# One PSUM bank for both query parts' sums, one for two second-layer products, two early score chunks in the ring banks, and new instruction orders

## The chip, the cores and the metric

The kernel runs on one core of a Trainium2 chip. The metric is device microseconds from start to end of one launch. Before the change the median of three runs is 324.44 us (324.27 to 324.97).

## What is computed

Attention for 8 batches, 8 heads, 576 queries of 64 elements, over 16 beacon keys and 576 causal keys; then a two-layer network on the 4,608 tokens, whose activation is h times the logistic function of 1.702 h.

```python
def _attn_ref(q, k, v, beacon_k, beacon_v):            # q, k, v: (8, 8, 576, 64)
    k_all = np.concatenate([beacon_k, k], axis=2)      # 16 beacon rows first
    v_all = np.concatenate([beacon_v, v], axis=2)
    scores = scale * np.matmul(q, k_all.transpose(0, 1, 3, 2))
    ...
    scores = np.where(causal, -1000000000.0, scores)
    a = np.exp(scores - scores.max(-1, keepdims=True))
    a /= a.sum(-1, keepdims=True) + 1e-09
    return np.matmul(a, v_all)
...
h = x @ w_in                                           # (4608, 512) @ (512, 2048)
g = h * (1.0 / (1.0 + np.exp(-1.702 * h)))
return g @ w_out                                       # (4608, 2048) @ (2048, 512)
```

## The kernel before

**Sets and chunks.** A set is four heads of one batch; there are 16. The scores of a set are kept transposed (keys on the partitions), only the blocks that the mask leaves, 1,664 columns for each head. They are made in 55 chunks (`CHUNKS`), of up to 512 columns for each of the four heads. For one chunk, PE runs 32-row matmuls (`e_qk`, L484) into four score banks of PSUM (tile s), and ScalarE takes the exponential of all four heads (`e_exp`, L495). The next chunk waits for that exponential, since there is one set of score banks (`chunk`, L933). Diagonal blocks are masked by GpSimd, those of the first halves of sets 0 and 1 by VectorE (`e_mask`, L509 and L516).

**Early and late sets.** Sets 0 to 3 are early: each half of the 288 queries has its own first chunk. Sets 4 to 15 are late and are worked off whole, in query parts of 224 and 352. For the softmax's denominators PE multiplies the exponentials by ones (`e_av` with x = 2, L571), for a late set after VectorE has added up the key blocks (`e_zadd`, L534). A late set's sums go to two ring banks, one for each query part. VectorE transposes each (`e_z1`, L583), takes reciprocals (L590) and transposes them back (`e_z2`, L594). The value products (`e_av` with x = 0 and 1, 32-column matmuls, L571) are multiplied by them into xT (`e_norm`, L606).

**The ring.** Four banks of PSUM, u0 to u3, are the ring: sums, value products, blocks of both layers all pass through them. An operation opens a bank, and its last reader closes it. After the last chunk the four score banks join the ring (`MORE`).

**The two layers.** Tokens go in groups of 256 (0 and 1) and 512 (2 to 9). The first layer runs in `e_m1` (L630), for groups 7 to 9 with seven products instead of eight (`e_part`, L831). The second layer is plain for groups 0 and 1 (`e_m2`, L675) and has seven products instead of eight for groups 2 to 9: `e_prod` (L744, 32 matmuls of 256 columns a product, in four operations), `e_half` (ScalarE, L755) and seven joins on VectorE (`e_join`, L760). Product 5 is joined twice, into u4 and into c22; c12 is u4 plus product 3. VectorE makes the products' left sides (`e_s`, L695).

**What sets the order.** `ORDER` lists for each engine the operations by number, the number being the place of the call of `op(...)` in the planning code. `Plan.run` follows the lists, gives every operation its ring bank, and the instructions are emitted engine by engine in that order. Each engine works off its own list in order. I call a PE operation score (mode r), value (c) or full (m); names are those of the planning code: qk7 is chunk 7, av1.2.0 the sums of set 1's first half (av1.0.0 and av1.1.0 its value products), m1.0.2 a block of group 0's first layer, m2.9.7.6 the last quarter of product 7 of group 9. On PE, the list of before begins:

qk0 qk1 av0.2.0 av0.0.0 av0.1.0 qk2 av1.2.0 av1.0.0 av1.1.0 qk3 m1.0.2 qk4 m1.0.0 qk5 m1.0.6 m1.0.4 av0.2.1 qk6 m1.0.8 m1.0.10 qk7 av0.1.1 m1.0.12 m1.0.14 m2.0.0.0 av1.2.1 av0.0.1 av1.0.1 av1.1.1 m2.0.0.1 m2.0.1.0 m1.1.0

On ScalarE: the exponentials of chunks 0 to 4 (chunks 0 and 1 in two instructions each), tanh twice, chunk 5, tanh twice, chunk 6. On VectorE: beacon cast, key transpose (the beacon's first), query transpose of set 0; the same of set 1; masks and normalisation of the first halves.

Of the kernel before, what the change touches and what calls it, by code (L numbers as in the profile page):

```python
# [7 lines left out]
F16 = mybir.dt.float16  # L8
# [9 lines left out]
        76, 100, 115, 118, 120, 106, 138, 141, 143, 108, 155, 111, 152, 129, 161, 158, 122, 131, 164, 167, 134, 127,  # L18
        170, 173, 176, 145, 125, 148, 150, 177, 182, 188, 191, 227, 194, 197, 232, 183, 203, 234, 200, 178, 237, 179,
        206, 258, 241, 209, 184, 263, 185, 212, 265, 213, 248, 246, 268, 214, 215, 401, 251, 253, 272, 218, 404, 275,  # L20
        244, 279, 219, 220, 407, 282, 284, 277, 221, 414, 320, 296, 304, 290, 302, 292, 300, 298, 312, 308, 294, 318,
        314, 310, 306, 316, 426, 435, 423, 343, 338, 339, 340, 433, 431, 438, 344, 345, 359, 349, 341, 464, 346, 350,
        351, 352, 354, 574, 355, 429, 360, 361, 577, 356, 362, 357, 372, 365, 583, 474, 477, 373, 366, 374, 367, 605,
        480, 484, 375, 482, 607, 368, 506, 502, 488, 492, 610, 490, 486, 498, 504, 500, 508, 514, 510, 516, 494, 496,
        512, 534, 593, 596, 535, 536, 539, 540, 550, 541, 542, 537, 742, 545, 546, 547, 548, 603, 745, 551, 552, 553,
        599, 601, 619, 622, 748, 555, 556, 557, 558, 561, 755, 625, 627, 629, 562, 563, 776, 568, 564, 569, 570, 571,
        779, 764, 767, 659, 637, 641, 657, 649, 651, 647, 661, 635, 631, 653, 805, 772, 770, 774, 643, 655, 633, 639,
        645, 679, 680, 815, 818, 700, 681, 682, 684, 701, 915, 690, 685, 686, 691, 692, 702, 918, 687, 693, 695, 703,
        696, 924, 821, 823, 697, 698, 706, 946, 825, 707, 713, 708, 709, 948, 934, 937, 714, 715, 716, 827, 951, 944,
        940, 942, 853, 831, 833, 855, 857, 851, 843, 835, 837, 847, 839, 845, 829, 849, 841, 1083, 960, 963, 875,  # L30
        876, 880, 877, 878, 881, 882, 1086, 968, 966, 970, 883, 1089, 902, 909, 903, 886, 891, 1096, 887, 888, 889,
        892, 893, 1117, 904, 894, 905, 896, 897, 1120, 898, 899, 910, 911, 1105, 1108, 1146, 912, 976, 994, 996, 972,
        978, 1000, 1002, 992, 984, 990, 986, 988, 974, 980, 982, 998, 1168, 1111, 1115, 1159, 1113, 1156, 1025, 1026,
        1020, 1027, 1171, 1021, 1022, 1028, 1023, 1031, 1177, 1032, 1033, 1164, 1166, 1162, 1199, 1034, 1036, 1047,
        1048, 1037, 1201, 1041, 1042, 1038, 1039, 1233, 1049, 1204, 1043, 1044, 1050, 1235, 1237, 1054, 1055, 1056,
        1057, 1239, 1249, 1190, 1241, 1265, 1251, 1242, 1253, 1255, 1187, 1245, 1267, 1258, 1281, 1257, 1269, 1216,
        1195, 1197, 1193, 1213, 1261, 1271, 1285, 1287, 1283, 1273, 1289, 1274, 1219, 1221, 1223, 1334, 1290, 1293,
        1277, 1357, 1335, 1313, 1318, 1314, 1336, 1315, 1319, 1316, 1320, 1321, 1373, 1324, 1325, 1337, 1326, 1329,
        1327, 1361, 1377, 1375, 1330, 1359, 1340, 1331, 1341, 1332, 1363, 1342, 1366, 1365, 1379, 1381, 1347, 1382,
        1348, 1369, 1389, 1385, 1349, 1343, 1395, 1393, 1391, 1405, 1350, 1397, 1398, 1409, 1437, 1407, 1411, 1413,  # L40
        1401, 1414, 1481, 1438, 1417, 1497, 1442, 1443, 1444, 1483, 1439, 1440, 1499, 1487, 1501, 1485, 1458, 1445,
        1459, 1460, 1489, 1513, 1490, 1448, 1453, 1449, 1450, 1451, 1454, 1503, 1455, 1493, 1505, 1461, 1456, 1464,
        1465, 1517, 1515, 1506, 1529, 1519, 1509, 1466, 1471, 1522, 1472, 1473, 1521, 1533, 1467, 1474, 1582, 1525,
        1535, 1537, 1531, 1538, 1561, 1566, 1562, 1541, 1588, 1567, 1589, 1563, 1564, 1568, 1569, 1572, 1590, 1573,
        1574, 1575, 1591, 1577, 1578, 1595, 1579, 1580, 1583, 1584, 1585, 1596, 1597, 1598,
    ],
    "ACT": [
        1, 3, 77, 79, 103, 101, 107, 109, 112, 153, 156, 130, 159, 162, 132, 165, 168, 135, 171, 174, 189, 192, 228,
        195, 198, 233, 235, 201, 204, 238, 180, 207, 259, 210, 264, 186, 266, 269, 216, 402, 405, 408, 222, 417, 415,
        297, 291, 303, 305, 301, 299, 293, 309, 321, 295, 319, 313, 315, 311, 307, 317, 436, 439, 342, 465, 468, 575,  # L50
        578, 584, 587, 606, 608, 503, 507, 489, 491, 493, 487, 499, 505, 509, 515, 517, 495, 501, 511, 497, 513, 611,
        538, 743, 746, 749, 756, 758, 777, 780, 660, 642, 638, 652, 658, 648, 650, 636, 632, 662, 654, 806, 644, 634,
        656, 640, 646, 809, 916, 683, 919, 928, 925, 947, 949, 952, 828, 832, 854, 856, 852, 858, 834, 838, 844, 840,
# [1304 lines left out]
```

## Time and profile before

| | |
|---|---|
| Median of three runs | 324.44 us |
| The profiled execution, and its span | 324.84 us, 323.1 us |
| Matmuls on PE | 4,508 |
| VectorE, ScalarE, GpSimd busy | 81%, 68%, 35% of the span |
| PE idle before its first matmul | 1.86 us |
| First score chunk, first first-layer matmul | 8.27 us, 17.21 us |
| Last matmul ends, last join ends | 319.06 us, 319.82 us |
| Loads of the first layer's weights land | 15.6 to 26.48 us |

The page gives each engine's busy time and its share of the span, and the span cut into 40 slices of some 8 us, with the busy share of each in tenths; the row PEclk is the clock that PE was granted. The chain of waits is the work that ended last, followed back from the end: start, length, engine, tile and line, and the number of matmuls merged into a piece. A row of the groups has line, engine, operation, what is written and read, the count, then busy time, the mean of one in ns, and the idle time ahead of them with what ended it. Timeline rows have start and length in us. Rows by window have busy times with instruction counts for PE, its weight loads, VectorE, ScalarE and GpSimd, then granted clock, DMA share and GB/s. PE's rows overlap, since matmuls are pipelined; the starts of single matmuls in the trace tell its pace.

### The profile page before, as it was taken

Reading aid. Unit: us, or ns where it says so; the run is one execution under the profiler, and the core shown is the slowest. Engines: PE = TensorE matmul, PEld = TensorE weight load, DVE = VectorE, ACT = ScalarE, POOL = GpSimd, SP = SyncE. Lnnn points to the kernel's source line nnn. Section 1 sums busy time; section 2 is a strip of 40 time slices with the busy share of each in tenths; the row PEclk is TensorE's granted clock in tenths of the full one; section 3 lists DMA queues with packets and bytes.
Section 4 is the critical chain, followed back from the end, with each engine's and each line's share of the span. In section 5 each row is a group of like instructions: output and inputs, shape, how many; then the busy total and the mean of one; then the engine's idle time right before and its main releaser. Section 6 shows DMA issues by size and latency. Waiting matters only on the chain. (4 is left out here: it accounts for less than half of the span.)

```text
span 323.1 us, 10371 instructions
## 1 busy us (share of the span) xinstructions
PE 312.2 (97%) x4508; PEld 230.0 (71%) x4508; DVE 261.7 (81%) x524; ACT 219.5 (68%) x272; POOL 113.4 (35%) x178
## 2 busy tenths in 40 slices
PE   7689999999999999999999999999999999999994
PEld 7467665644776467745878877646888888888884
DVE  4837798777987989976998889986999895585784
ACT  1676597677767686689767696768778735974830
POOL 8775478190328403871058208600221000000000
PEclk9899999999999999999999999999999999999998
DMA  7999999294423941396019908900111001101112
GB/s 124 163 200 208 206 185 184 54 97 85 123 70 66 185 73 34 53 183 89 2 36 134 189 3 80 176 28 2 37 34 65 4 32 34 67 2 36 65 67 97
DMA packets 58222, 28.85 MB, mean 89 GB/s; under 512 B 41280, under 2 KB 53568, under 8 KB 58176
## 3 DMA queue, kind: packets, MB, share of 16 engines
q0 software_dynamic: 47552, 18.49, 48.4%
q1 hardware_dynamic: 10560, 9.69, 9.3%
q8 instruction: 35, 0.57, 0.7%
q14 instruction: 11, 0.09, 0.1%
q10 hardware_dynamic: 64, 0.01, 0.0%
HBM read 37.22 MB, written 9.44 MB: 144 GB/s over the span
## 5 line engine op out<-in xcount | busy, mean ns | idle before, releaser
L495 ACT ACTIVATE E<-s 128x2048 f16<-128x2048 f32 (+5 forms) x66 | 98.9, 1515 | 41.4 <-PE s L484 40.9
L630 PE MATMUL u<-xT,w 128*128 128x256 f16 (+1 forms) x512 | 87.3, 326 | 0.6 <-ACT g L651 0.5
L516 POOL TENSOR_SCALAR_AFFINE_SELECT E<-E 128x512 f16<-128x512 f16 (+3 forms) x78 | 48.8, 658 | 107.5 <-ACT E L495 94.2
L630 PEld LDWEIGHTS <-w 128*128 128x128 f16 x512 | 49.0, 98 | 34.7 <-issue 1.9
L651 ACT ACTIVATE g<-u 128x512 f16<-128x512 f32 x80 | 43.2, 599 | 15.6 <-PE u L630 15.4
L744 PEld LDWEIGHTS <-g 128*128 128x128 f16 x512 | 48.5, 98 | 7.1 <-issue 0.3
L744 PE MATMUL u<-w,g 128*128 128x256 f16 x384 | 49.9, 273 | 0.0
L760 DVE SCALAR_TENSOR_TENSOR osb<-u,osb 128x512 f32<-128x512 f32 x56 | 37.6, 683 | 13.6 <-PE u L744 11.7
L484 PEld LDWEIGHTS <-kT 32*128 32x128 f16 x1376 | 25.6, 93 | 20.6 <-issue 12.1
L744 PEld LDWEIGHTS <-sA 128*128 128x128 f16 x384 | 36.3, 98 | 5.1 <-issue 0.3
L484 PE MATMUL s<-qT,kT 32*128 32x32 f16 (+20 forms) x1376 | 34.9, 230 | 3.9 <-ACT E L495 2.0
L859 ACT ACTIVATE g<-u 128x512 f16<-128x512 f32 x48 | 26.9, 602 | 12.4 <-PE u L831 6.8
L744 PE MATMUL u<-tB,sA 128*128 128x256 f16 x256 | 34.9, 273 | 0.1
L606 DVE TENSOR_TENSOR xT<-u,rz 128x352 f16<-128x352 f32 (+2 forms) x52 | 25.8, 518 | 7.4 <-PE u L571 7.1
L415 POOL DMA_DIRECT2D vb<-in_v_dram x32 | 27.4, 876 | 2.2 <-DMA qn<-in_q_dram 1.2
L571 PE MATMUL u<-E,vb 128*32 128x352 f16 (+8 forms) x928 | 27.9, 265 | 0.0
L534 DVE TENSOR_TENSOR zs<-zs,E 128x1344 f16<-128x1344 f16 (+2 forms) x36 | 22.6, 628 | 2.3 <-POOL E L516 1.6
L571 PEld LDWEIGHTS <-vb 128*32 128x32 f16 (+1 forms) x928 | 19.8, 97 | 5.5 <-issue 1.5
L455 DVE STREAM_TRANSPOSE kT<-kn 128x576 f32<-128x576 f32 x16 | 20.1, 1258 | 2.3 <-DMA kn<-in_k_dram 1.5
L831 PE MATMUL u<-xT,w 128*128 128x256 f16 x144 | 20.5, 273 | 0.0
L831 PEld LDWEIGHTS <-w 128*128 128x128 f16 x192 | 18.8, 98 | 2.2
L455 DVE STREAM_TRANSPOSE qT<-qn 128x576 f32<-128x576 f32 x16 | 19.9, 1241 | 0.1
(73 smaller groups left out, 397.5 us busy)
## 6 DMA issues: line engine op xcount, KB each, us to landing
out_dram<-osb SPq DMA_DIRECT2D x36, 256.0 KB, 2.3
kn<-in_k_dram POOLq DMA_DIRECT2D x16, 288.0 KB, 6.3
qn<-in_q_dram POOLq DMA_DIRECT2D x16, 288.0 KB, 6.8
vb<-in_v_dram POOLq DMA_DIRECT2D x24, 128.0 KB, 6.6
w<-in_moe_w_in_dram POOLq DMA_DIRECT2D x8, 256.0 KB, 9.6
w<-in_moe_w_out_dram POOLq DMA_DIRECT2D x4, 512.0 KB, 13.8
vb<-in_v_dram POOLq DMA_DIRECT2D x8, 112.0 KB, 5.0
vb<-in_v_dram POOLq DMA_DIRECT2D x8, 80.0 KB, 7.8
```

The lines of the kernel that those rows point to most:

```text
L415: nc.gpsimd.dma_start(out=t[0 : hi - lo, j, h0:h1, :], in_=v[b, h0:h1, lo:hi, :].rearrange("h n d -> n h d"),)
L455: nc.vector.transpose(out=f32(dst.rearrange("p n e -> p (n e)")).rearrange("p (r t) -> p t r", t=TR), in_=f32(src[:, :]).rearrange("p (t c ...
L484: nc.tensor.matmul(sc[:, h, o : o + w], kT[s % NB2][r : r + 32, j * P : (j + 1) * P, d], qT[s % NB2][r : r + 32, a : a + w, d], start=(d = ...
L495: nc.scalar.activation(out=Es[s][:, :, c0:c1], in_=ss[i][:, :, o : o + c1 - c0], func=AFT.Exp, scale=0.125,)
L516: nc.gpsimd.affine_select(out=blk, in_=blk, compare_op=ALU.is_ge, fill=0.0, base=off + (Nb if j == 0 else 0), pattern=[[0, Q], [1, w]], ch ...
L571: nc.tensor.matmul(u[32 * h : 32 * h + 32, a:e], lhs, src[0:kw, h, col : col + e - a], start=first, stop=last,)
L630: nc.tensor.matmul(u[:, o + a - t0 : o + e - t0], w1t[:, kp, nt * P : (nt + 1) * P], xT[:, kp, a % XR : (e - 1) % XR + 1], start=(kp == 0) ...
L651: nc.scalar.activation(out=gts[g][:, n0:n1, 0:w], in_=rings[("m1", g, n0)][:, 0 : n * w].rearrange("p (n w) -> p n w", n=n), func=AFT.Gelu ...
L744: nc.tensor.matmul(u[:, HM * mt : HM * (mt + 1)], lhs[:, n, mt * P : (mt + 1) * P], rhs[:, n, :], start=(n == 0 and mt == 0), stop=(n == H ...
L760: nc.vector.scalar_tensor_tensor(out=osbs[(g, dst)][:, :], in0=rings[("p", g, p)][:, :], scalar=scale_of(g), in1=osbs[(g, src)][:, :], op0 ...
L831: nc.tensor.matmul(u[:, HM * n : HM * (n + 1)], lhs[x][:, (2 * i + n) * P : (2 * i + n + 1) * P], rhs[:, x, :], start=fresh and n == 0 and ...
L859: nc.scalar.activation(out=gts[g][:, n : n + 2, HM * h : HM * (h + 1)], in_=rings[src][:, :].rearrange("p (n w) -> p n w", n=2), func=AFT. ...
```

## The change

**Sums.** A late set's sums of both query parts (now 288 and 288) go to one bank. The ones operand is 64 wide, with zeros in columns 32 to 47: with columns 32 to 63 a head's 32 output rows get the second part's sums in their last 16 rows and zeros in the first, and with columns 16 to 47 the first part's sums are added into the first 16. One transpose, one reciprocal over 18 columns (two rows of each 32) and one transpose of 576 columns follow. The transposed sums have a tile of their own, zt, for the whole kernel.

**Products.** Product 5 is joined once, into c22; then product 3 accumulates onto product 5 in the same bank, and c12 is u3's partner m plus that bank. The order is 1, 2, 6, 7, 5, 4, 3. A group has six joins. The four output tiles of a group are taken when its first is written.

**Early chunks.** Chunks 1 and 2 (the first half of set 1, the next part of set 0) write to four ring banks, one for each head, and each head has its own exponential, which closes the bank. Chunk 3 waits for chunk 0's exponentials alone. Chunk 1 is not split in two exponentials over all heads any more.

**Orders.** All lists are new. The PE list now begins (each "open" stands for a ring bank that a chunk takes and has no instruction):

qk0 open open open qk1 open qk3 open open qk2 qk4 av0.2.0 av1.2.0 av0.1.0 qk5 av1.0.0 av1.1.0 av0.0.0 av0.2.1 av0.0.1 qk6 m1.0.0 m1.0.2 qk7 m1.0.4 m1.0.6 m1.0.8 av0.1.1 av1.2.1 av1.0.1 av1.1.1 m1.0.10 m1.0.14 m1.0.12 m1.1.0

On ScalarE: chunk 0 (two), chunk 1 (four), chunk 3, two heads of chunk 2, chunk 4, two heads of chunk 2, chunks 5 and 6, tanh twice, chunk 7. On VectorE: query transpose, beacon cast and key transpose of set 0, cast and both transposes of set 1, one mask of set 1, three of set 0, two of set 1, then sums and products. GpSimd issues the query's load first, then the key's, those of set 1, a weight load, a query load of set 2, and the values. The end of the PE list is f9.3.4 and 24 operations of group 9's products, ending with product 3; VectorE's ends with eleven left-side differences of group 9 and one join among them, then five joins.

```diff
-    ones = cst.tile([P, 32], F16, tag="ones", name="ones")
+    ones = cst.tile([P, 64], F16, tag="ones", name="ones")
+    zt = cst.tile([P, HF], F32, tag="zt", name="zt")
+    nc.vector.memset(ones[:, 32:48], 0.0)
...
+    RINGED = (1, 2)
...
     def e_qk(i):
+        if i in RINGED:
+            ss[i] = [ring_tile(("qk", i, h)) for h in range(Q)]
...
         if x == 2 and s >= EARLY:
-            if half:
-                return [[2, P, 0, S - HA, zsum[s], HA - Z0, True, True, 0]]
             return [
-                [2, P, Z0, HA, zsum[s], 0, True, True, 0],
-                [2, P, 32, Z0, E, 32, True, True, 0],
-                [2, P, 0, 32, E, 0, True, True, 0],
+                [3, P, 0, HF, zsum[s], HF - Z0, True, False, 0],
+                [2, P, Z0, HF, zsum[s], 0, False, True, 0],
+                [2, P, 32, Z0, E, 32, False, True, 0],
+                [2, P, 0, 32, E, 0, False, True, 0],
             ]
...
+                    lhs = ones[0:kw, 32:64] if x == 3 else ones[0:kw, 16:48]
...
     def e_z2(s, half):
...
+        n = 1 if s < EARLY else 2
+        w = n * HF
...
-            out=rc[:, 0 : w // 32], in_=zt[:, 0:w].rearrange("p (b k) -> p b k", k=32)[:, :, 0]
+            out=rc[:, 0 : w // 32].rearrange("p (n b) -> p b n", n=n),
+            in_=zt[:, :].rearrange("p (b k) -> p b k", k=32)[:, :, 0 : 16 * n : 16],
...
     def e_prod(g, p, n0, n1):
-        u = ring_tile(("p", g, p))
+        u = ring_tile(("p", g, {3: 5}.get(p, p)))
...
-                    start=(n == 0 and mt == 0),
+                    start=(n == 0 and mt == 0 and p not in (3,)),
...
     def chunk(i):
...
-        if i:
-            deps += [exps[(i - 1, n)] for n in range(len(CHUNKS[i - 1]))]
+        if i in RINGED:
+            key = [("qk", i, h) for h in range(Q)]
+            plan.partial.update(key)
+            for x in key[1:]:
+                deps.append(op("PE", 0, list(deps), lambda: None, pr=0, ring=x, mode="r", name=f"open{i}"))
+        elif i:
+            k = max(x for x in range(i) if x not in RINGED)
+            deps += [x for (j, n), x in exps.items() if j == k]
...
+                    x = exps[(i, h)] = op(
+                        "ACT", 65 + 0.8345 * (c1 - c0), [qks[i]], lambda n=n, h=h: e_exp(i, n, h), pr=0, name=f"exp{s}.{i}",
+                        table="e", closes=key[h],
+                    )
...
-        prod(4)
-        c21 = join(4, "u", "b", [u3])
-        store(c21, "b", 1, 0)
-        prod(5)
-        u4 = join(5, "m", "m", [u3], False)
-        c22 = join(5, "u", "u", [c21, u4])
-        store(c22, "u", 1, 1)
-        prod(3)
-        c12 = join(3, "m", "m", [u4])
+        prod(5)
+        c22 = join(5, "u", "b", [u3], False)
+        store(c22, "b", 1, 1)
+        prod(4)
+        c21 = join(4, "u", "u", [c22])
+        store(c21, "u", 1, 0)
+        prod(3, 5, [c22])
+        c12 = join(3, "m", "m", [u3], at=5)
```

## The prediction

> **What bounds the kernel now.** I read the page's busy shares and slices first, then the chain of waits, then the starts of single matmuls in the trace, and last the timeline of the first 35 us.
>
> ```profile
> PE 312.2 (97%) x4508; PEld 230.0 (71%) x4508; DVE 261.7 (81%) x524; ACT 219.5 (68%) x272; POOL 113.4 (35%) x178
> ...
> PE   7689999999999999999999999999999999999994
> ...
> PEclk9899999999999999999999999999999999999998
> ```
>
> PE is busy from the fourth slice (24 us) to the last, so the time is PE's work plus what PE loses at the start and the end. A busy PE is not yet a PE at its peak; the chain shows what is lost inside:
>
> ```profile
> 224.14 1.85 PE u L744 x16
> 225.99 0.58 PE s L484 x22
> 226.57 2.29 PE u L744 x20
> ...
> 276.27 1.75 PE u L831 x16
> ...
> 304.65 2.18 PE u L831 x20
> ```
>
> Sixteen 256-column matmuls take 1.75 us between others of their kind and 1.85 before a score chunk (L484, 32-row pieces of the array); twenty take 2.18 and 2.29. Each change of form on PE costs 0.10 us. I matched the matmul records to the PE list. From an operation's first matmul to the next operation's, beyond its columns at the dense rate (1.75 us for 4,096), the median is 0.010 us for full to full, 0.103 for full to value (L571, 32-column pieces), 0.018 for value to value, 0.119 for value to full. After 34.40 us, where the first block of group 1 (m1.1.0) starts, this leaves only 2.7 us of true waits on PE in 284 us. So nothing off PE can give much there: only form changes, those 2.7 us, the start and the tail.
>
> **Form changes.** Decoded, the PE list has 133 changes of form from m1.1.0 on before, and 116 after: full to value 15 to 8, value to full 24 to 14, score to value 17 to 14, score to full 30 to 33, the others equal. The last two pairs cancel. What goes is 7 x 0.093 + 10 x 0.101 = 1.65 us, on the path (bounds 1.4 and 1.9 with single rows of 0.08 and 0.11). The columns stay: a late set's sums had 224 + 352 = 576 columns and have 288 + 288.
>
> **Sums in one bank, joined products: VectorE.**
>
> ```profile
> L760 DVE SCALAR_TENSOR_TENSOR osb<-u,osb 128x512 f32<-128x512 f32 x56 | 37.6, 683 | 13.6 <-PE u L744 11.7 <-ACT u L841 0.9 <-ACT osb L755 0.3
> L594 DVE STREAM_TRANSPOSE rz<-rc 128x352 f32<-128x352 f32 x12 | 6.5, 545 | 0.4
> L583 DVE STREAM_TRANSPOSE zt<-u 128x352 f32<-128x352 f32 x12 | 6.4, 536 | 0.6 <-PE u L571 0.6
> L594 DVE STREAM_TRANSPOSE rz<-rc 128x224 f32<-128x224 f32 x12 | 4.9, 411 | 0.4
> L583 DVE STREAM_TRANSPOSE zt<-u 128x224 f32<-128x224 f32 x12 | 4.9, 405 | 2.3 <-PE u L571 2.1
> ```
>
> A late set had two zt transposes (536 + 405), two reciprocals (219 + 187) and two rz transposes (545 + 411): 2.30 us. Now one zt of 288 columns (477, the early sets' row), one reciprocal of 18 columns (no row; 219 + 7 x 8 = 275 by the step from 7 to 11) and one rz of 576 (no row; 545 + 224 x 1.05 = 780 by the step from 224 to 352): 1.53 us. Twelve sets save 9.2 us. One join fewer in each of 8 groups saves 8 x 0.683 = 5.5 us. Together 14.7 us of VectorE's 261.7, worth nothing by themselves: PE runs beside them. What they can shorten is PE's 2.7 us of waits. Four of these stand before an operation that opens a new bank (m1.1.6 0.20, m2.2.4.0 0.28, m1.4.7 0.15, m1.6.0 0.16: 0.79 us). With a bank less per set in the ring of four I take half, -0.4 us; bounds -2.7 (none left) and +2.0 (a new order that waits about as often again).
>
> The join adds a wait: product 3 starts in product 5's bank only after the join that reads it. Product 4 stands between, 4 x 0.44 = 1.75 us; behind product 5 come at most two joins, 1.37 us, so it is hidden. Without product 4 it would cost some 0.9 us (1.37 - 0.44) in each group. In the last group, product 7's last part is the fifteenth PE operation behind the last first-layer product (14 x 0.437 = 6.1 us), and VectorE has until then one sum and two joins (0.65 apart) and eleven differences (0.36 apart): 0.2 + 1.95 + 3.96, and 0.1 until PE sees it, 6.2 us: +0.1 us. After PE's end a join and a store follow as before.
>
> **The early score chunks.** This is the uncertain term.
>
> ```profile
> 8.27 0.64 PE L484 MATMUL s<-qT,kT 32*128 32x288 f16 x24 [0.24 <-DVE qT L455]
> 8.98 1.94 ACT L495 ACTIVATE E<-s 128x1152 f16<-128x1152 f32 x2 [5.74 <-PE s L484]
> 11.36 0.64 PE L484 MATMUL s<-qT,kT 32*128 32x288 f16 x24 [1.39 <-DVE qT L455]
> 12.07 1.94 ACT L495 ACTIVATE E<-s 128x896 f16<-128x896 f32 x2 [1.15 <-PE s L484]
> 14.06 0.83 PE L484 MATMUL s<-qT,kT 32*128 32x288 f16 x24 [0.94 <-ACT E L495]
> 14.95 1.45 ACT L495 ACTIVATE E<-s 128x1536 f16<-128x1536 f32 x1 [0.94 <-PE s L484]
> ```
>
> The second chunk waits for VectorE's qT, not for the bank; the third is the first that waits for an exponential. I walk the new lists with these rows' durations:
> - The query is loaded and transposed first, so the beacon's cast and transpose (0.20 + 0.21, before at 3.64 and 3.87 in the shadow of the load) stand between the two transposes. The first chunk starts at 8.6 instead of 8.27, the second at 11.47 instead of 11.36.
> - The second chunk's exponential is four of 512 columns (0.594 each, 2.38 instead of 1.94) and ends at 14.6 instead of 14.0. The fourth chunk goes into the score banks meanwhile, so ACT goes on without its bubbles of 0.94: chunk 3 ends at 16.0 and chunk 4 at 18.5 (before 18.8 and 20.9). ACT gains 1.5 to 2 us.
> - But chunk 2 takes all four ring banks from 14.6 on, until its own exponentials (0.49 each, behind chunk 3's) free one at 16.5. So the first sums start at 16.6 instead of 12.16, and the chain zt, rc, rz and products, 4.0 us on VectorE, ends at 21.1 instead of 17.7. The order also puts chunk 6 before the first layer, and it waits for an exponential that ends at 21.05. The first layer begins at 21.6 instead of 17.21; with PE under half clock up to then (below) I take 22.2.
> - From there to m1.1.0 PE has 8 blocks (7.0 us), a chunk (0.5), four value operations (2.2) and changes (0.5): 10.2 us, so m1.1.0 starts at 32.4. Before it started at 34.40, but behind three second-layer operations (0.96 + 0.88 + 0.86 = 2.70) that the new order has later: 31.70 to compare. The start loses 0.7 us.
> Loads do not decide: the first layer's weights land from 15.6 to 26.5 before, and one query load more ahead of them (1.4 us) brings the last to 27.9, two blocks before its use. Bounds: -1.0 (norms at 20.5, full clock), +3.0 (one more stretch under half clock, 1.7, and VectorE's gates and the third set's transposes late by 0.6).
>
> **Sum.** -1.65 - 0.4 + 0.1 + 0.7 = -1.25 us. The profiled execution took 324.84 us (span 323.1 and 1.7 around it), 0.4 above the median of 324.44; the sum is of its rows and taken from the median: **323.2 us**. About 0.2%, 0.65 us, is what a measurement of this kernel tells from no change.
>
> **Rivals.**
> 1. The start gains. The exponentials run 2 us ahead, and if the norms end near 20.5 at full clock the start gives 1.0 instead of taking 0.7: 324.44 - 1.65 - 0.4 + 0.1 - 1.0 = 321.5. For it: the 0.94 bubbles. Against: two chunks on four ring banks are not "idle banks", since the sums need them. Chance 0.15.
> 2. The start eats the gain: VectorE late with the gates (+0.6) and no fewer waits (+0.4): 324.2. This is also the case that the change does not do what it says, since the second ring chunk only waits for the first. Chance 0.15.
> 3. Slower: the clock. Between 8 and 14 us PE has little to do, and then its granted clock falls:
>
> ```profile
> 12.00:14.00 2.00, 0.96 (x37) 0.70 (x37) 1.45 (x7) 1.93 (x2) 1.64 (x3) 0.98 1.14 149
> 14.00:16.00 2.00, 1.94 (x56) 1.54 (x59) 1.95 (x5) 1.06 (x2) 0.11 (x1) 0.50 1.75 171
> 16.00:18.00 2.00, 1.77 (x41) 1.35 (x34) 1.52 (x4) 1.06 (x2) 1.77 (x3) 0.67 1.54 190
> ```
>
> That is 0.08 + 2.0 + 1.32 = 3.4 us at half clock (the granted clock is the third column from the end). After, PE is thinner from 8 to 21 us, and a second and third such stretch would end at 24. On small operations it costs little, on dense first-layer blocks half of it: 1.7 us, and the gates wait with it (+0.6): 324.44 - 1.25 + 1.7 + 0.6 = 325.5. It decides from the point at which the clock is below 1.00 after 22 us. Chance 0.22.
> The Trainium skill, "TensorE: Matmul & The Clock Gate", section "Part 1: The HAM clock gate", says that an idle window of about 3.4 us halves the clock and a busy one restores it; the 3.4 us above agree, and by that rule this rival's time follows if no window before 22 us counts as busy.
>
> **Chances.** Forecast 0.48 (own range 322.3 to 324.1, of which 0.38 is faster by over 0.2% and 0.10 within), rival 1 0.15 faster, rival 2 0.12 within and 0.03 slower, rival 3 0.22 slower. Faster 0.53, same 0.22, slower 0.25. The range from 321.2 to 326.0 takes in rival 1, and rival 3 with half a stretch more.
>
> **What would show it.** Full-to-value and value-to-full changes at 0.10 each and 17 fewer; m1.1.0 near 32.4 us with no second-layer operation ahead of it; the first sums at about 16.6; VectorE near 247 us; waits on PE behind m1.1.0 summing to 2 to 3 us. Wrong would make it: m1.1.0 before 31 or after 34, or waits on PE above 4 us, which would mean that the new orders hold PE where I could not see it.

## The result, and the profile after

The changed kernel is slower: 326.88 us in the median of six executions (326.22 to 327.74), before 324.43 in six beside it, a ratio of 1.0073 with an interval of 1.0053 to 1.0094. The profiled execution took 326.28 us with a span of 324.5; before it was 324.84 and 323.1. The profiles thus differ by 1.44 us and the medians by 2.45.

The page of the changed kernel, the same rows as were shown of before:

```profile
PE 310.2 (96%) x4508; PEld 230.6 (71%) x4508; DVE 247.3 (76%) x481; ACT 220.3 (68%) x277; POOL 117.9 (36%) x178
...
PE   6499999999999999999999999999999999999995
...
PEclk9969999999999999999999999999999999999999
```

PE has 2 us less to do and VectorE 14.4 us less, and still the end is later. The first slices say where to look: PE had 7 and 6 tenths in them before and has 6 and 4 now, and its granted clock dips to 6 tenths, in the third slice, where before it dipped to 8, in the second. The groups of the changed kernel, one row for each shape (line, engine, operation, tiles, count, then busy time and mean ns):

```profile
L770 DVE SCALAR_TENSOR_TENSOR osb<-u,osb 128x512 f32<-128x512 f32 x48 | 32.8, 684 | 16.8 <-PE u L754 15.5 <-PE u L582 0.5 <-ACT osb L767 0.3
L592 DVE STREAM_TRANSPOSE zt<-u 128x288 f32<-128x288 f32 x20 | 9.4, 468 | 4.0 <-PE u L582 3.9
L603 DVE STREAM_TRANSPOSE rz<-rc 128x576 f32<-128x576 f32 x12 | 9.3, 778 | 0.4
L598 DVE RECIPROCAL rc<-zt 128x18 f32<-128x18 f32 x12 | 3.2, 263 | 0.1
```

Eight joins fewer, one transpose of 468 ns where two stood, 778 and 263 ns for the two shapes that had no row: VectorE's share came out as priced. The rows of PE and ScalarE in the first 17 us of the changed kernel (start, length):

```profile
9.00 0.64 PE L491 MATMUL s<-qT,kT 32*128 32x288 f16 x24 [1.61 <-DVE kT L458]
11.85 0.64 PE L491 MATMUL u<-qT,kT 32*128 32x288 f16 x24 [1.15 <-DVE qT L458]
12.54 2.07 ACT L502 ACTIVATE E<-u 128x512 f16<-128x512 f32 x4 [0.89 <-PE u L491]
14.66 0.54 PE L491 MATMUL u<-qT,kT 32*128 32x288 f16 x24 [1.81 <-ACT E L502]
16.00 0.83 PE L491 MATMUL s<-qT,kT 32*128 32x208 f16 x32 [0.80 <-ACT E L502]
16.76 0.58 PE L582 MATMUL u<-E,ones 128*32 128x288 f16 x8
```

The first sums start at 16.76 (before 12.16). What follows them is in the chain of the changed kernel's start (start, length, what):

```profile
9.80 8.49 DMA vb<-in_beacon_v_dram
18.29 0.14 issue
18.42 0.62 PE u L582 x11
...
30.56 3.49 PE u L640 x30
```

The beacon's values, which GpSimd issues at 9.80 behind a weight load and a query load, land at 18.29, and the third value operation, av0.1.0, stands until then. Before they were there by 12.6 us. From 18.42 on nothing but PE's own work is on the chain: what is late here stays late.

The windows of the changed kernel (the granted clock is the third column from the end):

```profile
14.00:16.00 2.00, 0.54 (x24) 0.42 (x24) 1.29 (x5) 2.00 (x4) 1.29 (x3) 0.95 2.39 152
16.00:18.00 2.00, 1.80 (x56) 1.37 (x55) 0.95 (x4) 1.83 (x3) 1.99 (x4) 0.50 1.67 181
18.00:20.00 2.00, 1.58 (x44) 1.09 (x48) 1.52 (x5) 1.24 (x4) 1.99 (x4) 0.50 1.59 193
20.00:22.00 2.00, 2.00 (x60) 1.57 (x56) 1.84 (x5) 1.31 (x1) 2.00 (x4) 0.50 1.24 207
22.00:24.00 2.00, 2.00 (x58) 1.56 (x51) 1.63 (x6) 0.51 (x1) 0.84 (x2) 0.85 1.24 204
```

The clock is halved from 15.8 to 22.6 us, 6.83 us instead of 3.41. The first layer starts at 23.34 (17.21 before) and m1.1.0 at 33.24, 1.54 us behind the comparable 31.70.

Behind m1.1.0 I matched the records to the list as in the prediction. There are 116 form changes (133 before) with the same medians, 0.103, 0.119, 0.018 and 0.010 us. The waits sum to 4.86 us; before they summed to 2.75. The view of waits on PE from 33 us to 320 us (waiting line, releaser: total, times, longest) shows the largest:

```profile
PE u L582 <- DVE osb L770: 1.0, 2, 0.6
PE u L841 <- DVE u L863: 0.6, 1, 0.6
PE u L640 <- ACT g L661: 0.4, 1, 0.4
PE u L582 <- issue: 0.3, 1, 0.3
```

Before, the same view had only the third of these (0.5). The first two are new: PE waits for VectorE to read a bank. The chain around the longest:

```profile
124.86 0.82 DVE zs L541
125.67 0.60 DVE osb L770
126.27 0.51 DVE zs L541
126.94 0.18 issue
127.12 0.69 DVE osb L770
127.86 1.00 PE u L582 x33
```

The list has av6.0.0 av6.1.1 av6.0.1 av7.2.0 in a row. Each opens a bank after 0.3 to 0.6 us, and each bank is free only when VectorE has read it: a join of 0.69 us, queued behind additions of set 7's sums (zs). PE stands 0.79 us before av6.0.1, and in the same way 0.57 before av5.0.0 and 0.72 before f7.0.3 (there the sum of the last block is queued behind additions).

### The profile page after: what moved, and what is told of

It is laid out like the page before. It is cut to its first block, busy times and chain, and to the rows that moved or that the text cites. A ratio compares the mean times of both kernels' runs of the same rounds, so it can differ in the third digit from the quotient of the medians.

```text
span 324.5 us, 10329 instructions
## 1 busy us (share of the span) xinstructions
PE 310.2 (96%) x4508; PEld 230.6 (71%) x4508; DVE 247.3 (76%) x481; ACT 220.3 (68%) x277; POOL 117.9 (36%) x178
## 4 chain that ended last, share of the span: by engine, by line
PE 85%; DMA 5%; ACT 3%; DVE 3%; POOL 2%; issue 1%; DVEq 0%; POOLq 0%
PE u L754 31%; PE u L640 24%; PE u L841 11%; PE u L582 9%; PE s L491 7%; DMA vb<-in_beacon_v_dram 3%; PE u L685 2%; DMA kn<-in_k_dram 2%; ACT E L502 1%; DVE osb L770 1%; DMA vb<-in_v_dram 1%; ACT L661 1%; DVE zs L541 1%; POOL E L523 1%; DVE tB L705 0%
## 5 line engine op out<-in xcount | busy, mean ns | idle before, releaser
L502 ACT ACTIVATE E<-s 128x2048 f16<-128x2048 f32 (+5 forms) x63 | 95.6, 1532 | 44.0 <-PE s L491 43.7
L523 POOL TENSOR_SCALAR_AFFINE_SELECT E<-E 128x512 f16<-128x512 f16 (+2 forms) x78 | 53.6, 706 | 95.8 <-ACT E L502 95.6
L640 PEld LDWEIGHTS <-w 128*128 128x128 f16 x512 | 49.2, 98 | 32.8 <-issue 1.2
L770 DVE SCALAR_TENSOR_TENSOR osb<-u,osb 128x512 f32<-128x512 f32 x48 | 32.8, 684 | 16.8 <-PE u L754 15.5
L491 PEld LDWEIGHTS <-kT 32*128 32x128 f16 x1376 | 24.8, 94 | 22.4 <-issue 13.3
L491 PE MATMUL s<-qT,kT 32*128 32x32 f16 (+20 forms) x1328 | 33.7, 230 | 2.4 <-DVE kT L458 1.6
L582 PE MATMUL u<-E,vb 128*32 128x288 f16 (+8 forms) x928 | 28.4, 269 | 2.0 <-DVE osb L770 1.0
L582 PEld LDWEIGHTS <-vb 128*32 128x32 f16 (+1 forms) x928 | 20.5, 99 | 7.9 <-issue 3.0
L705 DVE TENSOR_TENSOR sA<-g 128x512 f16<-128x512 f16 x32 | 13.0, 417 | 13.3 <-ACT g L661 13.2
```

Of the source, the lines that this page charges most:

```text
L491: nc.tensor.matmul(ss[i][h][:, o : o + w], kT[s % NB2][r : r + 32, j * P : (j + 1) * P, d], qT[s % NB2][r : r + 32, a : a + w, d], start=( ...
L502: nc.scalar.activation(out=Es[s][:, :, c0:c1] if h is None else Es[s][:, h, c0:c1], in_=sall[i][:, :, o : o + c1 - c0] if h is None else s ...
L523: nc.gpsimd.affine_select(out=blk, in_=blk, compare_op=ALU.is_ge, fill=0.0, base=off + (Nb if j == 0 else 0), pattern=[[0, Q], [1, w]], ch ...
L582: nc.tensor.matmul(u[32 * h : 32 * h + 32, a:e], lhs, src[0:kw, h, col : col + e - a], start=first, stop=last, skip_group_check=s >= EARLY ...
L640: nc.tensor.matmul(u[:, o + a - t0 : o + e - t0], w1t[:, kp, nt * P : (nt + 1) * P], xT[:, kp, a % XR : (e - 1) % XR + 1], start=(kp == 0) ...
L770: nc.vector.scalar_tensor_tensor(out=osbs[(g, dst)][:, :], in0=rings[("p", g, p)][:, :], scalar=scale_of(g), in1=osbs[(g, src)][:, :], op0 ...
```

## The experiments

**The ledger.** Each kernel was laid out as the prediction's sum, against before. *Start* is the start of m1.1.0 less the second-layer operations ahead of it (31.71 before); *forms* are the form changes behind it, at 0.10 us; *waits* are what remains there of the gaps between operations. The columns give the differences from before, then their sum, the measured shift of the last matmul's start, all from the one profiled execution of each kernel, and last the ratio on record, which is of the mean times of the executions, not of their medians.

| Kernel | start | forms | waits | sum | measured | ratio |
|---|---|---|---|---|---|---|
| changed kernel | +1.53 | -1.70 | +2.11 | +1.93 | +1.68 | 1.0073 |
| key_first | +1.60 | -1.70 | +2.64 | +2.55 | +2.29 | 1.0053 |
| values_first | +1.34 | -1.70 | +1.97 | +1.61 | +1.35 | 1.0036 |
| waits_fixed | +0.97 | -1.80 | +2.38 | +1.55 | +1.30 | 1.0043 |
| spread_values | +0.93 | -1.30 | +0.98 | +0.60 | +0.33 | 1.0050 |
| start_spread | +0.81 | -1.30 | +0.96 | +0.47 | +0.20 | 1.0009 |
| start_spread_2 | +0.81 | -1.30 | +1.42 | +0.93 | +0.65 | 1.0017 |
| old_80 | +0.24 | -1.40 | +3.33 | +2.17 | +2.00 | 1.0057 |
| mended | +0.13 | -1.00 | +1.43 | +0.55 | +0.36 | 1.0000 |
| mended_2 | +0.58 | -1.00 | +1.74 | +1.32 | +1.13 | 1.0010 |
| new_start | +4.99 | 0.00 | -0.13 | +4.86 | +4.79 | 1.0138 |
| new_80 | +2.75 | -0.30 | +4.94 | +7.39 | +7.23 | 1.0156 |
| old_start | 0.00 | -1.70 | +6.20 | +4.50 | +4.35 | 1.0142 |
| old_order | +0.39 | -0.30 | +11.81 | +11.89 | +11.68 | 1.0344 |
| products_alone | +0.15 | 0.00 | +12.75 | +12.90 | +12.90 | 1.0368 |

In all fifteen the three terms give the measured shift to within 0.3 us. That is less of a test than it looks: the waits are what is left of the gaps, so that the sum nearly closes by construction. It shows that the columns stay the same, that 0.10 us for a form change holds on the whole, and which of the three terms moved. For these, the sizes of two were wrong in the prediction.

**old_start and new_start: the start alone, both ways.** My first theory was that the start makes the loss.

```diff
 old_start: changed kernel, RINGED = (), every list of before up to m1.1.0, the new lists behind it
 new_start: before with RINGED = (1, 2), the new lists up to m1.1.0, before's lists behind it
```

> The changed kernel, but with everything up to m1.1.0 as before: no score chunk in the ring banks, and on each engine the old list's operations of the start, then the rest of the new lists. Theory (the new start costs 1.5 us: m1.1.0 at 33.24 us after, against 34.40 less 2.70 for the three second-layer operations behind which it stood before): m1.1.0 near 31.7 to 32.0, and 325.3 us in the median. Rival (the middle alone, the waits on PE behind m1.1.0, 4.9 us after and 2.7 before, makes the whole loss): the time stays at 326.9.

> The kernel before with the new start alone: chunks 1 and 2 in the ring banks and the new lists up to m1.1.0, then the old lists, sums in two banks and seven joins as before. Theory (start costs 1.5 us): 325.9 us against 324.4 before, PE granted less clock up to 23 us than before. Rival (the middle alone): 324.4.

Both missed: 329.35 us (ratio 1.0142, interval 1.0123 to 1.0160) and 329.44 us (1.0138, 1.0117 to 1.0159). The first restored the start (m1.1.0 at 34.40 with 2.69 us of second layer ahead), and then lost 6.2 us more in waits than before had, most of it within 15 us behind the joint; the first and longest of these waits, 1.55 us, stands there because the new lists count on a query load of set 2 that the old start issues later. The second had the first sums at 16.66, 6.83 us at half clock, and m1.1.0 at 39.39. Its first second-layer operation starts at 33.81, and then PE waits:

```profile
37.67 1.89 PE L682 MATMUL u<-w,g 128*128 128x512 f16 x8 [2.83 <-DMA w<-in_moe_w_out_dram]
```

The second layer's weights, which the new start issues later, are not there when before's list wants them. Up to this wait, with the changed kernel's list of PE, the new start is 2.1 us behind the comparable 31.71, where my theory had 1.5; 0.35 us of the difference is a wait for VectorE's normalisation. Cut at that place, the two orders don't fit each other, so neither time gives the start a clean price.

**key_first: the order of the first two loads.** The query is loaded ahead of the key; this turns it round.

```diff
-GpSimd: load query 0, load key 0, ...     VectorE: query transpose, beacon cast, ...
+GpSimd: load key 0, load query 0, ...     VectorE: beacon cast, key transposes, ...
```

> The changed kernel with set 0's key loaded and transposed ahead of its query, as before; nothing else. If the beacon's cast and transpose between the two transposes are what delays the first chunk (9.00 us after, 8.27 before), it starts 0.4 us earlier and, as the chunks hang on it, the time falls by 0.3 to 0.5 us to 326.4. If the late landing of the first load (6.09 us after, 5.51 before) delays it, only a part of this shows. If the start hangs on the values' loads instead (first value product at 18.42 us, just when the beacon's values land at 18.29), the time stays.

326.13 us, ratio 1.0053 (1.0030 to 1.0076). The first chunk starts at 9.01 as in the changed kernel (9.00): the key landed at 5.44, but now the query landed at 7.68. In this execution the order of these two loads is not where the time went. One trace says little of it: with the same two loads in this order the query landed at 7.68 and 7.71 in two kernels and at 7.00 in two others, and the first chunk started at 9.0 in the former and at 8.3 in the latter. The median of 326.13 takes in one execution of 332.82; the other eleven have 326.05, and the ratio is of these.

**waits_fixed: four places, for the three largest waits.**

```diff
 VectorE: -zadd7 zadd7 join3(u2)      +join3(u2) zadd7 zadd7
 VectorE: -zadd zadd sum22.7 sum21.7  +sum22.7 sum21.7 zadd zadd      -t norm2  +norm2 t
 TensorE: -qk25 m2.2.4.6              +m2.2.4.6 qk25
```

> The changed kernel with four places of its lists turned round, where its trace shows PE waiting for VectorE's order: group 3's second join ahead of two additions of set 7 (PE waited 0.79 us), the first sums of the split first layer ahead of two additions of sets 14 and 15 (0.72), a product of set 2 ahead of a weight difference (0.30), and a quarter of group 2's product 4 ahead of a score chunk (0.57). Theory (these waits stand on PE's path): 1.2 to 2.0 us less, 325.2 us. Rival (they only move, since later places wait for the same engine): 326.5 or more.

326.32 us, ratio 1.0043 (1.0029 to 1.0057), waits 5.13 us. The time lies just under the rival's 326.5 us and well above the theory's 325.2, and the waits moved as the rival says. They now stand before av2.0.0 (1.03 us), av5.0.0 (0.67), av7.2.0 (0.89) and av14.2.0 (0.39): all of them value operations that open a bank.

**old_80 and new_80: a cut at 80 us**, where both lists have issued the same 92 operations.

```diff
 old_80: changed kernel, RINGED = (), lists of before up to set 4's first operation, the new lists behind it
 new_80: before with RINGED = (1, 2), the new lists up to there, before's lists behind it
```

> The changed program (one-bank sums, joined products) with the order of before on every engine up to set 4's first operation on TensorE, about 80 us, where both orders have issued the same 92 operations; from there the new order. The early chunks in the ring banks are out. Theory A, the first 80 us make the loss: in the profiles the operation qk20 starts 1.15 us later in the changed kernel, and the rest adds 0.53 us (1.4 us saved in form changes, 1.9 us added in waits), so this kernel should stand 0.5 us above before: ratio 1.0016, range 0.999 to 1.003, with first sums near 12.2, first layer-1 product near 17.2, half clock near 3.4 us, and qk20 within 0.4 us of before's. Theory B, the later part makes the loss: ratio 1.005 or more, and qk20 where before has it.

> Before's program (sums in two banks, seven products joined) with the early chunks in the ring banks and the new order up to set 4's first operation on TensorE, the old order behind it. Theory A: 1.15 us above before, ratio 1.0035, range 1.002 to 1.006, with half clock of about 6.8 us, first sums near 16.7, and the offset against before at qk20 about the same as that at the end. Theory B: within 0.2% of before.

The kernel old_80 took 326.62 us (1.0057, 1.0045 to 1.0070) and new_80 330.15 us (1.0156, 1.0133 to 1.0178). At qk20 old_80 stands where before does (-0.17 us), so its loss comes behind 80 us; by the letter that is theory B. But a part of it is the joint; the waits on PE of old_80 from 78 to 82 us:

```profile
PE u L581 <- DVE zs L540: 0.9, 1, 0.9
```

The additions of set 4 stand too late on VectorE there. The rest of the new order costs 1.08 us from qk23 to the end, 0.41 in the changed kernel itself. In new_80 the joint costs 2.69 us at once, and then the clock. The wait stands inside av4.2.0, whose second piece needs a mask that GpSimd has not made yet:

```profile
85.32 0.23 PE L578 MATMUL u<-E,ones 128*32 128x80 f16 x8 [2.51 <-POOL E L523]
```

The windows around it:

```profile
82.00:84.00 2.00, 0.81 (x8) 0.21 (x6) 1.74 (x4) 1.95 (x4) 2.00 (x4) 1.00 1.48 128
84.00:86.00 2.00, 0.68 (x32) 0.55 (x31) 1.93 (x5) 0.58 (x1) 1.75 (x4) 1.00 1.06 138
86.00:88.00 2.00, 1.83 (x27) 1.15 (x16) 1.86 (x8) 1.79 (x1) 0.00 (x0) 0.64 1.27 187
88.00:90.00 2.00, 2.00 (x11) 1.18 (x8) 2.00 (x4) 0.09 (x1) 1.35 (x2) 0.51 1.46 193
```

From 86.6 to 90.0 PE runs at half clock: each second-layer piece of 0.44 us takes 0.86. From qk19 to qk23 the kernel falls 4.2 us further behind before.

**spread_values and values_first: the two causes in the changed kernel, one at a time.**

```diff
 spread_values
 TensorE: -av5.1.1 av5.0.0        +av5.1.1 m2.2.3.0 av5.0.0
 TensorE: -av6.0.1 av7.2.0        +av6.0.1 m2.3.4.4 qk31 av7.2.0
 VectorE: the join and the sums as in waits_fixed, the weight difference t left in its place
 values_first
 GpSimd: -query 0, key 0, key 1, query 1, weights, query 2, values 0 (four), beacon values
 GpSimd: +key 0, query 0, key 1, query 1, beacon values, values 0 (three), query 2, value 0, weights
```

> The changed kernel with its clusters of value products taken apart by one other operation each: m2.2.3.0 between av5.1.1 and av5.0.0, m2.3.4.4 and qk31 between av6.0.1 and av7.2.0, and on VectorE the join that closes their bank ahead of two additions of set 7, and the last block's sums ahead of two additions. Theory: the waits before av5.0.0 (0.57), av6.0.1 (0.79) and f7.0.3 (0.72) shrink by 1.5 us together, two to four more form changes cost 0.2 to 0.4: 1.2 us below the changed kernel, ratio against before 1.0035, waits after m1.1.0 about 3.4 us. Rival: the waits only move to the next operation that opens a bank: ratio 1.006 to 1.008, waits 4.5 us or more.

> The changed kernel with the key loaded first and the mask and the values of the first blocks loaded ahead of the weight load and of set 2's query. Theory: av0.1.0 no longer waits for its values at 18.4 us, and the first layer-1 product and m1.1.0 come 0.8 to 1 us earlier (first layer-1 product near 22.4): ratio 1.0045. Rival: the half clock lasts 6.8 us all the same and VectorE's chain sets the first layer-1 product: it stays at 23.3 and the ratio at 1.007; or the weights, now later, stop layer 1 and the ratio is above 1.009.

The waits of spread_values fell to 3.73 us (theory about 3.4, rival 4.5 or more) for four form changes more, and the last matmul's shift from 1.68 to 0.33; of these 1.35 us, 0.60 came from the start, whose lists had not been touched. It was the two changed places of TensorE that took the waits away: waits_fixed has the same two moves on VectorE, and its waits rose. The new list has short waits of its own, 0.21 before qk27, 0.41 before qk33 and 0.39 before av14.2.0. The median did not follow: 326.59 us (1.0050, 1.0030 to 1.0069), between the theory's 1.0035 and the rival's 1.006, the executions lying between 324.75 and 328.00 and the profiled one, at 324.95, being one of the fastest. In values_first the beacon's values landed at 10.59, av0.1.0 started at 17.97 instead of 18.42, and m1.1.0 at 33.05: only 0.2 us earlier, since PE then stands inside the chunk qk6, between its 11th and its 12th matmul:

```profile
22.13 0.42 PE L491 MATMUL s<-qT,kT 32*128 32x192 f16 x11
22.87 0.35 PE L491 MATMUL s<-qT,kT 32*128 32x160 f16 x13 [0.33 <-issue]
```

From the 11th start to the 12th go 0.49 us, and the changed kernel has no such stop. The view names no wait for it. It stands at the same matmul in start_spread (0.74 us), start_spread_2 (0.94), key_first (1.02) and new_80 (1.35), and in all five it ends 1.3 to 1.6 us after a 16 KB load of the queue that the page calls instruction has landed (21.49 us here). So it is likely that PE stops for its own instructions there, and that this bounds how early qk6 can end; no run tried it. The median of values_first fell to 325.95 (1.0036, 1.0022 to 1.0049). The ratio is the theory's or better (1.0045), while the first layer's start, 23.16, lies nearer the rival's 23.3 than the theory's 22.4.

**start_spread: both together**, and f7.2.2 ahead of av14.2.0.

> The changed kernel with both the loads of values_first and the places of spread_values (and one more, f7.2.2 ahead of av14.2.0). Theory, the two add up: 0.9 us from the start and 1.2 us from the waits: ratio 1.001, range 0.999 to 1.003. Rival: they do not add up and the kernel stays where values_first stands: ratio 1.0035 or more.

325.05 us, ratio 1.0009 (1.0000 to 1.0019): the theory. Of the changed kernel's 2.45 us most are gone, all but some 0.3 by the ratio, with the same sums, products and chunks and an order that differs in a few places. How the two changes share this is not shown: m1.1.0 starts at 32.52, 0.53 us earlier than in values_first with the same loads and lists up to there, in an execution in which the query landed 0.7 us earlier.

**mended: before's first 80 us, the new rest with its value products apart.**

```diff
 old_80 with  VectorE: before's list up to set 4's fourth addition, that addition two places earlier
              TensorE, VectorE: the places of spread_values, f7.2.2 ahead of av14.2.0
```

> The kernel old_80 (before's order for the first 80 us, then the new one) with its joint mended (VectorE keeps before's order up to the fourth addition of set 4, 0.98 us of waiting in old_80) and with the clusters of value products taken apart as in spread_values. Theory: 326.6 us of old_80 less 0.9 for the joint and 1.2 to 1.9 for the waits: ratio 0.998, range 0.9965 to 1.000, waits after m1.1.0 below 3.5 us. Rival: a wait that is taken away comes back at the next operation that opens a bank: ratio 1.002 or more.

324.78 us, ratio 1.0000 (0.9991 to 1.0009), the slow end of the theory's range, with waits of 4.18 us, above the 3.5 that it named. All of the loss is gone and nothing is gained. Ten form changes fewer (-1.0) stand against 1.43 us of waits more. Its waits on PE:

```profile
PE u L639 <- ACT g L660: 0.5, 1, 0.5
PE s L490 <- ACT E L501: 0.3, 1, 0.3
PE u L753 <- DVE osb L769: 0.2, 1, 0.2
PE u L840 <- DVE zt L591: 0.2, 1, 0.2
```

The first is before's own; the others are short and of several kinds.

**old_order and products_alone: the new forms in before's order.**

```diff
 old_order: changed kernel, RINGED = (), before's lists; of the late sets' two sums the later place is kept (set 14: the earlier);
            products 5, 4, 3 fill the twelve places of 4, 5, 3 in each group; set 15's last norm ahead of group 7's first join
 products_alone: before with the joined products alone, the same lists with both sums
```

> The sums in one bank and the joined products, both in before's order; the early chunks and the new order are out. Only what the new forms force is moved: the one product of the sums stands where the later of the two stood, and of the three last products of a group the one that goes on in the bank of another takes the last places. Theory A, the new order and its start make the loss and the new forms cost nothing: ratio 0.999, range 0.997 to 1.002, with waits on TensorE after m1.1.0 of 2 to 3.5 us and as many form changes as before. Rival: the third product must now wait for the join that reads the bank in which it goes on, 0.69 us and a queue on VectorE in each of eight groups: waits above 5 us, ratio 1.007 or more.

> Before's program with the joined products alone, in before's order; the sums stay in two banks and seven sets of sums stay as they were. It differs from the kernel old_order by the sums alone. Theory A: ratio 0.999 to 1.002, the same as old_order within 0.15%, since what the sums save on VectorE (some 10 us) lies beside TensorE's work. Rival: VectorE's 10 us matter, and this kernel stands 0.5% or more above old_order.

335.98 us (1.0344, 1.0331 to 1.0358) and 336.56 us (1.0368, 1.0352 to 1.0384): the rival, and more. In old_order PE waits 0.94, 1.80 and 0.80 us before product 3 of groups 4, 5 and 9, where the join that reads the shared bank is not yet done: product 4 stands between here too, but on VectorE the join stands behind additions and normalisations (in group 4 it ends at 170.87 and product 3 starts at 170.93). 3.2 us more go in five waits (0.35 to 0.95) before other products and values that open a bank. Some 5.6 us belong to group 7: there the norm that had to move makes PE wait 0.74 and 3.15 us, and the clock follows. Its windows:

```profile
264.00:266.00 2.00, 0.00 (x0) 0.00 (x0) 2.00 (x7) 0.00 (x0) 0.00 (x0) 1.00 0.00 0
266.00:268.00 2.00, 1.31 (x11) 1.15 (x12) 0.63 (x2) 0.00 (x0) 0.00 (x0) 0.94 0.00 0
268.00:270.00 2.00, 2.00 (x12) 1.41 (x10) 0.00 (x0) 0.00 (x0) 0.00 (x0) 0.50 0.00 0
270.00:272.00 2.00, 2.00 (x15) 1.58 (x14) 0.00 (x0) 0.60 (x1) 0.00 (x0) 0.71 0.00 0
```

PE has no matmul for two whole microseconds, and at 267.8 the clock is halved for 3.41 us. So the shared bank needs an order made for it: in before's order the waits ahead of product 3 alone are 3.5 us. The two kernels differ by 0.6 us, and products_alone had 6.83 us of half clock at that place: what the sums in one bank, 9 us of VectorE, are worth beside it these two runs don't tell.

**mended_2 and start_spread_2: four waits more.**

```diff
 VectorE: -zadd12 join5 zadd12 turn14 join5   +join5 zadd12 zadd12 join5 turn14
 TensorE: -qk33 m1.4.9     +m1.4.9 qk33        -qk27 m2.2.3.6   +m2.2.3.6 qk27
```

> The kernel mended with four more waits taken apart: on VectorE the joins of products 2 and 6 of group 5 stand ahead of an addition and a transpose, and on TensorE m1.4.9 and m2.2.3.6 stand ahead of the score chunks qk33 and qk27 that they followed. Theory, waits and form changes are separate terms: mended's waits of 4.18 us fall by 0.8 to 1.2 and the kernel is the first below before: 324.0 us of before's 324.8, ratio 0.9975, range 0.996 to 0.9985. Rival, the waits are bound up with the clusters that save the form changes and only move: ratio 0.9995 to 1.002, waits 4 us or more.

> The same four moves in the kernel start_spread, which has the changed kernel's start and waits of 3.71 us, of which two of the four (m2.2.3.4, 0.21, and m2.3.5.6, 0.41) are among these. Theory: 0.4 to 0.6 us below start_spread: ratio 0.9995, range 0.998 to 1.001. Rival: ratio 1.001 or more.

325.43 us (1.0010, 1.0002 to 1.0019) and 325.51 us (1.0017, 1.0008 to 1.0026): the rival in both. The waits rose to 4.49 and 4.17 us. Those before qk27 (0.21), qk33 (0.41) and, in mended_2, m2.5.5.0 (0.38) and m1.6.9 (0.21) are gone; in their place 0.24 stands before qk28, 0.45 before m1.3.8 (0.26 in mended), 0.66 before qk34 and, in mended_2, 0.45 before av12.2.0.

## Why the prediction was wrong, step by step

**The bound: right.** PE's list is the kernel: in fifteen kernels start, forms and waits, all read from PE's own records, give the start of the last matmul to within 0.3 us. The waits are a remainder there, so this says where the time is lost and not why.

**Form changes: right**, 17 fewer at 0.10 us, -1.65 predicted and -1.70 in the ledger.

**VectorE: right.** 247.3 us for a forecast of 247, 263, 778 and 468 ns for 275, 780 and 477, and nothing gained by it. Product 3's wait is hidden in the changed order, as predicted: no wait above 0.15 us stands before one. The step "at most two joins behind product 5" holds only for VectorE's new order: in old_order product 4 stands between as well, and the wait is 0.80 to 1.80 us in three groups, because other work stands ahead of that join.

**The bank relief, -0.4 us: wrong in sign.** It measured +2.1, just outside its upper bound of +2.0. I counted banks per set and did not ask in which order they are opened. Fewer form changes means that value operations stand next to one another, and such a row opens banks in 0.3 to 0.6 us each that VectorE frees in 0.5 to 0.7 each. Spreading two such rows on TensorE took 1.1 us of waits away for four form changes, shown by spread_values. I had also read the four waits of before one place off: they were named by the operation before the gap, but the operation that waits is the next one. Three of the four next ones (m2.2.6.0, m1.4.5, m1.6.9) do open a bank; behind m1.1.6 it is qk9, a score chunk, which opens none. So 0.59 of the 0.79 us were waits for banks. My own sign of being wrong came: waits above 4 us.

**The start, +0.7 us: mis-sized, +1.54 measured.** The first sums (16.6 forecast, 16.76 measured) and the chunks were well placed. "Loads do not decide" failed: I had followed the weights' loads and not the beacon's values, which the new list puts behind a weight load and a query load. That the chain of the end runs over this landing is shown above; values_first shows that 0.45 us of it comes back at av0.1.0 and 0.2 us at m1.1.0, where the stop inside qk6 takes the rest. The first layer then began 1.1 us later than forecast. With the same loads and the same lists up to there, m1.1.0 lies at 33.24 in the changed kernel and at 32.63 and 32.68 in spread_values and waits_fixed: half clock ends at 22.6 us in the first and at 21.5 in the other two. Some 0.1 to 0.2 us of this difference is there at av0.1.0 already, so 0.4 to 0.5 of the 1.54 may lie with where the stretch falls (argued from three traces, not tried by itself). Against it, key_first has half clock only to 20.3 us and gains nothing: it has qk6 1.0 us earlier than the changed kernel, loses 1.02 us inside it and has m1.1.0 at 33.31. The rest I leave undivided: the first sums come 4.6 us later, no run undid the chunks in the ring alone, and m1.1.0 differs by up to 0.6 us between kernels with the same start.

**Rival 3, the clock: it came, and was priced too high.** The clock was below 1.00 behind 22 us, its deciding point, and the time is on its side; but in the profiled executions the mechanism carries a small part. In 77 executions of before, beside the experiments, those with a mean granted clock of 0.997 or more (33) have a median span of 323.0 us. Those at 0.990 or less (20) have 323.4; at a span of 323 us that is some 6 to 7 us at half clock (an estimate: 0.010 of it, times two). Where in these executions it lay is not traced. The kernel old_80 had 6.83 us at half clock and m1.1.0 at only +0.24 us. I had said 1.7 and 0.6. The Trainium skill, "TensorE: Matmul & The Clock Gate", section "Part 1: The HAM clock gate", adds that the window which decides runs freely, so that the phase differs from run to run; the traces agree, with the same start and half clock from 15.8 us in one kernel and from 14.7 in two others.

**The tail: right.** The +0.1 us was a wait before product 7's last part, and 0.09 us stands there. Behind the last matmul, where I had forecast no change, the end is 0.26 us shorter: the span grew by 1.42 us and the last matmul's start by 1.68.

**The range** ended at 326.0 because I took the upper bounds of start and waits one at a time. Both terms came out high together.

**Open.** The medians differ by 2.45 us and the profiles by 1.44. With the changed kernel's loads the executions spread over 1.5 us (the changed kernel) and 3.3 us (spread_values), and the two kernels with the values first have medians 0.9 and 1.5 us lower, which is more than their traces show; but waits_fixed, with the changed kernel's loads, spreads over 0.6 us only, and key_first, with its own order of loads, over 3.9 us. Part of the spread goes with the clock. Four executions of spread_values with a mean granted clock of 0.984 or less took 326.59 to 328.00 us, the other seven 324.75 to 326.75; the changed kernel's longest, 327.74, and the two longest of key_first's eleven, 328.74 and 329.50, stand at 0.983 and 0.984. Yet waits_fixed and values_first have executions at 0.982 that are not longer than their others. Whether the clock or the values' landing makes the spread, and so the 1 us by which the medians differ more than the profiles, is not shown. Also open is whether any order turns the saved form changes into time: no kernel here lies below before, and waits taken away came back in waits_fixed, mended_2 and start_spread_2.

## What to carry to other kernels

When TensorE is full, write the change as a ledger of start, form changes and waits, and bound the waits by asking for every row of short operations whether their banks are freed as fast as they are opened. A rule that groups operations of one form to save 0.10 us a change pays with waits when each of them opens a bank. When a list of loads is set anew, follow every load to its first reader, the small ones too, and add the upper bounds of terms that can go wrong together.

## What the runs showed of the hardware

A wait of PE can cost more than itself: after PE had been idle for 2.51 us (new_80) and for 2.99 us (old_order, group 7) it ran at half clock for 3.41 us, some 1.7 us more. But its length alone does not decide: 1.80 us (old_order, group 5) brought no such stretch, and neither did 2.83 us in new_start, where the granted clock stays at 1.00 from 34 to 40 us.

The price of half clock depends on what lies under it. On dense second-layer work it doubles each 0.44 us piece. At the start, where PE waits for VectorE and ScalarE anyway, old_80 had 6.83 us of it and was only 0.24 us later at m1.1.0.

The start of one kernel is not the same from one execution to the next: with the same loads the query landed at 7.68, 7.71, 7.01 and 7.00 us in four kernels, and their first chunks started 0.7 us apart.
